# Routing lists of a mixture-of-experts kernel: when the first gathers, the one-hots and the list products are issued

## The chip, the cores and the metric

The kernel runs on one core of one Trainium2 chip. Its time is the device time of one execution in microseconds (us). An execution has five instruction streams: TensorE (PE, with its weight loads as PEld), VectorE (DVE), ScalarE (ACT), GpSimd (POOL) and SyncE (SP, which here only issues transfers). Each stream runs in order; between streams, semaphores make one wait for another.

## The reference

Block-diagonal attention (chunks of 64 positions, 8 heads of 64) makes a matrix x of 4608 tokens by 512. A mixture of 8 experts follows, in which each token goes to one expert only:

```python
logits = x @ w_gate + modality_bias[modality_id]      # 4608 x 8
e_idx = argmax(logits, axis=1)
gate_w = softmax(logits)[arange(N), e_idx]
for e in range(8):
    mask = e_idx == e
    h = maximum(x[mask] @ w1[e], 0)                   # 512 -> 1024
    out[mask] = gate_w[mask, None] * (h @ w2[e])      # 1024 -> 512
```

All is in f32. The matrix products of the experts take three products each, since every factor is split into a high and a low part.

## The kernel before

**Attention.** The tokens come as 36 tiles of 128, worked off in pairs (`a` = 2, 4, ... 34). For a tile, `scores` makes the products of q and k, `exps` and `sums` the softmax, `transposes` and `values` the product with v, and `rows` turns the result back to token rows and makes the logits in the same product; `put` stores the rows to the scratch tensor `xd`. `rows` and `put` of a pair run one pair later than its `values`.

**Slots.** The experts' work is cut into slots: 11 wide ones of 384 tokens (three tiles), then slots of 256. Slots 0 to 12 always run. Slots 13 to 21 stand in nested branches (`rest`) and run only if the routing needs them. Each slot has one expert, and a list says which rows of `xd` belong to it. `gather` fetches these rows by an indirect transfer that POOL issues, one for each tile. For slot 0 the rows are transposed on PE and split (`split`); for later slots they go through a scratch tensor (`stash` and `place`, on SP's queue), DVE transposes blocks of 32 (`turn`), and `part` splits them. A slot has eight slices f = 0 to 7 of the hidden width: `first` makes the hidden slice (PE, then ACT writes its high part hh and DVE its low part hl), `second` adds its product to the output in PSUM. PE runs `first(f)` and then `second(f-1)`, so that hh and hl of a slice have the time of a `second` and a `first` to be made. `wsplit(g+4)` splits the weights of the slice that is four ahead (ACT wh, DVE wl). `finish` scales the outputs and scatters them (POOL).

**Lists.** The tokens are routed in two groups, tiles 0 to 13 (early) and 14 to 35 (late). The early group's lists serve slots 0 to 2 and are made during attention (`early_table`). Tokens of the early group that these slots don't take, and the late group, go into the late lists, for slots 3 and above. A list is made by a matrix product: a one-hot matrix for each tile (`hots`, `late_hots`: POOL compares a row of 0 to 127 with each token's place in its block of 128), times a matrix that has the token's number and gate in the column of its block (a match `eq`, which DVE makes, times `parts`; the lists' products on POOL or DVE). `slot_table` (DVE, some 60 small operations) works out which expert each slot has.

**Order.** The order on each engine is the program's, written by hand. `PLAN` says what is issued after which tile (key -7 is tile 29), `PREP` what is issued in which slice of slots 0 to 2. The routing and the lists are generators in two lists, `jobs` and `pooljobs`. `advance` (line 866) takes each to its next `yield`: first all in `jobs`, then all in `pooljobs`. It is called once for each tile of attention, and in a slot three times a slice: after `first`, after `wsplit`, and after `second` and that slice's `PREP`. Numbered from the start of slot 0, slice f has the advances 3f+1, 3f+2 and 3f+3. The late group's `route` enters the list at advance 1 (its `heads` run then on DVE and POOL); its maximum at advance 3 (`gmx`, line 344), its one-hot `oh` and the prefix sums `scan` at advances 4 and 5 (lines 357 to 366), the gates at 5; then it passes five yields, and the two rank products `rp` (PE, lines 388 and 389) come at advance 10, in slice 3. `slot_table` takes advances 11 to 29, one step each, and `late_lists` follows, with 13 more: in each, a match for four tiles, its product with `parts`, and, four advances behind, four matrix products into `ll` (PE, line 462). `settle` in slice 7 of slot 1 runs down what is left, and `gather 3` follows it.

What an advance issues stands in the engines' in-order streams at that place: PE meets the products `rp` between `first` and `second` of a slice.

Of the kernel before, what the change touches and what calls it, by code (L numbers as in the profile page):

```python
# [26 lines left out]
NT = N // P  # L27
# [3 lines left out]
NTT = SLOT // P  # L31
NWIDE = 11
NSURE = NWIDE + 2
MAXSLOT = 22
BUSY = 4
PLAN = {
    -9: {"fetch": [(0, 1), (1, 1)]},
    -13: {"heads": [(14, 4)]},
    -11: {"heads": [(18, 4)]},
    -7: {"gather": [(0, (0,))], "heads": [(22, 4)]},  # L40
    -6: {"hi": [(0, 0)]},
    -5: {"gather": [(0, (1, 2))], "heads": [(26, 4)], "lo": [(0, 0)], "hi": [(0, 1)]},
    -4: {"fetch": [(2, 1)], "lo": [(0, 1)], "hi": [(1, 0)]},
    -3: {"fetch": [(3, 1)], "heads": [(30, 2)], "lo": [(1, 0)]},
    -2: {"hi": [(1, 1)]},
    -1: {"fetch": [(4,)], "lo": [(1, 1)]},
    0: {"gather": [(1,)], "rank": [()], "hi": [(2,)], "lo": [(2,)]},
}

PREP = {  # L50
# [9 lines left out]
NEARLY = 3  # L60
# [8 lines left out]
NEG = 1  # L69
# [17 lines left out]
C_END = C_TH2 + NJ2  # L87
NBLK = NEARLY * NTT
NTAIL = TAIL // P
NLATE = (NWIDE - NEARLY) * NTT + (MAXSLOT - NWIDE) * NTAIL  # L90
PART = 4


@with_exitstack
def attention_moe(ctx: ExitStack, tc: tile.TileContext, qkv, mod, cst, bias, wcat, wfst, out):
    nc = tc.nc
    V, A, PE, G, SP = nc.vector, nc.scalar, nc.tensor, nc.gpsimd, nc.sync

# [10 lines left out]
    NB, NV = 4, 6  # L109
# [196 lines left out]
    def heads(t0, n, e):  # L306

        a = t0 - GROUPS[1][0]
        l0, lg = lps[1][:, a:a + n], late[:, a:a + n]
        e.tensor_tensor(l0, l0, ris[:, t0:t0 + n].unsqueeze(3).to_broadcast([P, n, H, E]), ALU.mult)  # L310
        lh = wk.tile([P, 4, H // 2, E], F32, name="lh4")[:, 0:n]
        G.tensor_tensor(lh, l0[:, :, 0:4], l0[:, :, 4:8], ALU.add)
        G.tensor_tensor(lh[:, :, 0:2], lh[:, :, 0:2], lh[:, :, 2:4], ALU.add)
        G.tensor_tensor(lg, lh[:, :, 0], lh[:, :, 1], ALU.add)
        G.tensor_tensor(lg, lg, mb[:, t0:t0 + n], ALU.add)
# [4 lines left out]
    def route(g):  # L320
        t0, n = GROUPS[g]
# [60 lines left out]

        if g >= NEG:
            gates()
        for _ in range(2 if g < NEG else 5):
            yield
        rp = ps.tile([P, 2, 32, E], F32, tag="s" if g < NEG else "t", name="rp")
        PE.matmul(rp[:, 0, 0:n], ub, oh, start=True, stop=True)
# [20 lines left out]
            gates()  # L409
            return  # L410
        blocks(pf, pbl[:, ts], blkl[:, ts])
        ready.add("ranks")
        jobs.append(slot_table())

    def blocks(row, low_, high):

        n = row.shape[1]
        pi = wk.tile([P, n], I32, name="pi")
        V.tensor_copy(pi, row)
        V.tensor_single_scalar(pi, pi, P - 1, ALU.bitwise_and)  # L420
        G.tensor_copy(low_, pi)
        G.tensor_tensor(high, row, low_, ALU.subtract)
# [9 lines left out]

    late_hot = []

    def late_hots():

        for t in range(NT):
            if t == n0:
                while "ranks" not in ready:
                    yield  # L440
            if t % 16 == 0:
                b = wk.tile([P, 2, DM], F32, name="qk", bufs=NB).rearrange("p a b -> p (a b)")
                late_hot.append(b.bitcast(BF16).rearrange("p (t b) -> p t b", b=P))
            G.tensor_scalar(late_hot[t // 16][:, t % 16], place_, pbl[:, t:t + 1], None, ALU.is_equal)
            if t % 3 == 2:
                yield
        ready.add("late hot")

    def rank():
        pooljobs.append(late_hots())  # L450

    tkl = cp.tile([P, NLATE], I32, name="tkl")
    gatel = cp.tile([P, NLATE], F32, name="gatel")

    def late_lists(to):

        whats = []
        lt = None

        def product(c):  # L460
            for t in range(c * PART, (c + 1) * PART):
                PE.matmul(lt.rearrange("p b c -> p (b c)"), late_hot[t // 16][:, t % 16],
                          whats[c][:, t % PART], start=(t == 0), stop=(t == NT - 1))

        lag = 4
        for c in range(NT // PART + lag):
            if c < NT // PART:
                tp = slice(c * PART, (c + 1) * PART)
                eq = wk.tile([P, PART, NLATE], BF16, name="eq4")
                V.tensor_tensor(eq, blkl[:, tp].unsqueeze(2).to_broadcast([P, PART, NLATE]),  # L470
                                to.unsqueeze(1).to_broadcast([P, PART, NLATE]), ALU.is_equal)
                w = wk.tile([P, DM], F32, name="v", bufs=NV) if c < NV else wk.tile([P, H, 64], F32, name="ex", bufs=4).rearrange("p a b -> p (a b)")
                w = w.bitcast(BF16)[:, 0:PART * NLATE * 5]
                (V if c % 3 == 2 else G).tensor_tensor(  # L474
                    w.rearrange("p (t b c) -> p t b c", t=PART, c=5),
                    eq.unsqueeze(3).to_broadcast([P, PART, NLATE, 5]),
                    parts[:, tp].unsqueeze(2).to_broadcast([P, PART, NLATE, 5]), ALU.mult)
                whats.append(w.rearrange("p (t m) -> p t m", t=PART))
            if c >= lag:
                if lt is None:  # L480
                    assert "late hot" in ready
                    lt = ps.tile([P, NLATE, 5], F32, tag="t", name="ll")
                product(c - lag)
            yield
        ls = wk.tile([P, NLATE, 5], F32, name="lls", bufs=1)
        V.tensor_copy(ls, lt)
        V.scalar_tensor_tensor(ls[:, :, 0], ls[:, :, 0], float(OOB), ls[:, :, 1], ALU.add, ALU.add)
        V.tensor_copy(tkl, ls[:, :, 0])
        V.tensor_tensor(ls[:, :, 2], ls[:, :, 2], ls[:, :, 3], ALU.add)
        V.tensor_tensor(gatel, ls[:, :, 2], ls[:, :, 4], ALU.add)  # L490
        ready.update(("list", i) for i in range(NEARLY, MAXSLOT))

    taken = cp.tile([P, E], F32, name="taken")

# [3 lines left out]
    def early_table(blk, pf, oh, fm):  # L498
# [49 lines left out]
        V.tensor_tensor(ls[:, :, 2], ls[:, :, 2], ls[:, :, 3], ALU.add)  # L548
        V.tensor_tensor(gate9, ls[:, :, 2], ls[:, :, 4], ALU.add)
        ready.update(("list", i) for i in range(NEARLY))  # L550
        yield
        yield
        gone = wk.tile([P, n0, E], F32, name="gone", bufs=1)
        G.tensor_tensor(gone, oh, taken.unsqueeze(1).to_broadcast([P, n0, E]), ALU.mult)
        first_ = wk.tile([P, n0], F32, name="first", bufs=1)
        V.tensor_scalar(first_, fm, -float(CAP), float(E * CAP), ALU.mult, ALU.add)
        yield
        yield
        left_ = wk.tile([P, n0], F32, name="leftrow", bufs=1)
# [2 lines left out]
        V.tensor_tensor(first_, left_, first_, ALU.is_lt)  # L562
        V.scalar_tensor_tensor(left_, first_, -float(2 ** 20), left_, ALU.mult, ALU.add)
        blocks(left_, pbl[:, 0:n0], blkl[:, 0:n0])

    def slot_table():
        def t1(name, shape):
            return wk.tile([P] + shape, F32, name=name, bufs=1)
# [85 lines left out]
        pn = t1("pn", [W3, NTT])  # L654
        V.tensor_tensor(pn, y[:, 0:W3, E:E + 1].to_broadcast([P, W3, NTT]), bcm(pen, W3, NTT), ALU.mult)
        th3 = thr.rearrange("p (a b) -> p a b", a=NTT)[:, :, 0]
        to = t1("tol", [NLATE])
        for a, r0, r1, m in ((0, 0, W3, NTT), (W3 * NTT, W3, R, NTAIL)):
            V.tensor_tensor(to[:, a:a + (r1 - r0) * m].rearrange("p (a b) -> p a b", b=m),
                            row[:, r0:r1].unsqueeze(2).to_broadcast([P, r1 - r0, m]),  # L660
                            bcm(th3[:, 0:m], r1 - r0, m), ALU.add)
        t3 = to[:, 0:W3 * NTT]
        V.scalar_tensor_tensor(t3, pn.rearrange("p a b -> p (a b)"), -1000.0, t3, ALU.mult, ALU.add)
        jobs.append(late_lists(to))

    def listed(s):
        if s < NEARLY:
# [51 lines left out]
    def split(k, tag="t"):  # L719

        hi, lo = xring[0]
        tp = ps.tile([P, 512], F32, tag=tag, name="tp")[:, 0:SLOT]
        for t in range(NTT):
            assert ("rows", 0, t) in ready
            PE.transpose(tp[:, t * P:(t + 1) * P], xg[:, t, k * P:(k + 1) * P], ident)
        A.copy(hi[:, k], tp)  # L726
        V.tensor_tensor(lo[:, k], tp, hi.bitcast(F32)[:, k], ALU.subtract)  # L727
# [138 lines left out]
    def advance(lists=None):  # L866
        for js in lists or (jobs, pooljobs):
            for j in list(js):
                if next(j, "end") == "end":
                    js.remove(j)  # L870

    ctx.enter_context(tc.manual_schedule())
    ahead = {"rank": rank, "heads": lambda t, n: heads(t, n, G), "gather": gather, "stash": stash, "place": place, "turn": turn, "part": part, "settle": settle, "fetch": fetch, "hi": whi, "lo": wlo, "lo1": wlo}
    def plan(k):
        for what, calls in PLAN.get(k, {}).items():
            for a in calls:
                ahead[what](*a)
# [44 lines left out]
    put(NT - 2)  # L922
    split(2)
    split(3)
    plan(0)

    def last():
# [78 lines left out]
```

## Time and profile before

| | |
|---|---|
| median of three runs | 571.75 us (571.51 to 572.02) |
| profiled execution, device time | 573.04 us |
| its span in the profile | 571.3 us |
| PE busy in the span | 556.2 us (97%) |
| DVE busy | 374.6 us (66%) |
| ACT busy | 244.7 us (43%) |
| POOL busy | 188.2 us (33%) |

The profile is of one execution. Its device time is 1.74 us over its span and 1.29 us over the median of the runs. A row of a timeline gives the start, the duration, engine, line, operation and how many were merged; in brackets stands how long the engine was idle ahead of it and what ended that. A row of the windows gives a stretch, its length, busy time of each engine with its count of instructions, the clock granted to TensorE (1.00 is full), the share of DMA in use and GB/s.

### The profile page before, as it was taken

The numbers are of one execution on the slowest core, as the hardware profiler recorded it, in microseconds if no ns is written. First come the engines' busy times: TensorE is split into PE (matmuls) and PEld (weight loads), VectorE is DVE, ScalarE is ACT, GpSimd is POOL, SyncE is SP. The second block draws the span as 40 slices with busy tenths as digits, with TensorE's granted clock in tenths as the row PEclk, the third lists the DMA queues.
The fourth block names the chain that finished last, engine by engine and source line by source line (L and its number), as shares of the span: only waits on it lengthen the run. The fifth ranks groups of instructions, "written<-read, shape, count | busy, mean of one in ns | idle before, by whom it ended". The sixth has DMA issues, their size and how long they took to land.

```text
span 571.3 us, 12435 instructions
## 1 busy us (share of the span) xinstructions
PE 556.2 (97%) x4950; PEld 502.8 (88%) x4950; DVE 374.6 (66%) x655; ACT 244.7 (43%) x422; POOL 188.2 (33%) x244
## 2 busy tenths in 40 slices
PE   8999999998999899999999999999999999999995
PEld 6999999997889689989899898989989988998894
DVE  4767799886899785565655556565655656556751
ACT  3554555464444233343434434344343444434541
POOL 3322556674899745022040402204040210302011
PEclk9999999998999899999999999999999999999999
DMA  9999998987779428758486766839666573755510
GB/s 332 325 304 303 305 309 286 315 319 262 221 245 290 157 94 246 301 173 279 147 290 203 221 225 180 275 134 306 205 210 232 154 273 126 258 185 180 207 38 26
DMA packets 52755, 130.55 MB, mean 229 GB/s; under 512 B 5198, under 2 KB 22734, under 8 KB 46288
## 3 DMA queue, kind: packets, MB, share of 16 engines
q1 hardware_dynamic: 40864, 100.68, 54.3%
q0 software_dynamic: 5920, 18.88, 8.9%
q10 hardware_dynamic: 5904, 10.11, 4.9%
q8 instruction: 41, 0.67, 0.5%
q14 instruction: 26, 0.21, 0.1%
HBM read 102.12 MB, written 28.05 MB: 228 GB/s over the span
## 4 chain that ended last, share of the span: by engine, by line
issue 49%; PE 28%; POOL 11%; DVE 5%; DMA 5%; ACT 2%; POOLq 0%; ACTq 0%; DVEq 0%
PE yb L793 7%; PE hp L780 7%; POOL xg L685 5%; PE sp L242 4%; PE yb L289 4%; PE xp L277 3%; POOL out L805 3%; PE ap L263 2%; DMA qk<-in_qkv 2%; DMA xg<-xd,tk 1%; DMA v<-in_qkv 1%; DVE eq L470 1%; DVE xr L291 1%; POOL ex L474 1%; ACT ex L251 1%
## 5 line engine op out<-in xcount | busy, mean ns | idle before, releaser
L757 DVE TENSOR_TENSOR wl<-raw,wh 128x1024 fp32r<-128x1024 f32 (+1 forms) x106 | 128.1, 1210 | 33.9 <-ACT wh L753 33.7
L783 ACT ACTIVATE hh<-hp 128x384 fp32r<-128x384 f32 (+1 forms) x104 | 49.4, 475 | 225.7 <-PE hp L780 223.0
L780 PE MATMUL hp<-xh,wh 128*128 128x384 f32 (+1 forms) x416 | 137.0, 329 | 0.0
L780 PE MATMUL hp<-xh,wl 128*128 128x384 f32 (+1 forms) x416 | 136.8, 329 | 0.0
L780 PE MATMUL hp<-xl,wh 128*128 128x384 f32 (+1 forms) x416 | 136.3, 328 | 0.2 <-DVE xl L727 0.2
L784 DVE SCALAR_TENSOR_TENSOR hl<-hp,hh 128x384 fp32r<-128x384 f32 (+1 forms) x104 | 55.6, 534 | 106.4 <-ACT hh L783 106.1
L793 PE MATMUL yb<-wh,hh 128*128 128x512 f32 x296 | 118.3, 400 | 0.3 <-ACT hh L783 0.3
L793 PE MATMUL yb<-wh,hl 128*128 128x512 f32 x296 | 117.4, 397 | 0.0
L793 PE MATMUL yb<-wl,hh 128*128 128x512 f32 x296 | 117.2, 396 | 0.0
L805 POOL DMA_INDIRECT out<-yo,tkl x28 | 28.1, 1002 | 248.7 <-DVE yo L804 243.1
L753 ACT CAST wh<-raw 128x1024 fp32r<-128x1024 f32 (+1 forms) x106 | 108.5, 1025 | 0.2 <-issue 0.2
L780 PEld LDWEIGHTS hp<-xh,wh 128*128 128x128 f32 x416 | 78.4, 188 | 4.3 <-ACT xh L726 0.3
L780 PEld LDWEIGHTS hp<-xl,wh 128*128 128x128 f32 x416 | 78.3, 188 | 4.1 <-DVE xl L727 0.4
L780 PEld LDWEIGHTS hp<-xh,wl 128*128 128x128 f32 x416 | 78.2, 188 | 0.0
L793 PEld LDWEIGHTS yb<-wh,hl 128*128 128x128 f32 x296 | 55.8, 189 | 14.3 <-DVE hl L784 0.5
L793 PEld LDWEIGHTS yb<-wh,hh 128*128 128x128 f32 x296 | 56.0, 189 | 9.7 <-ACT hh L783 0.8
L793 PEld LDWEIGHTS yb<-wl,hh 128*128 128x128 f32 x296 | 55.9, 189 | 9.6
L252 POOL TENSOR_TENSOR sr<-ex 128x256 f32<-128x256 f32 x36 | 26.2, 729 | 63.5 <-ACT ex L251 63.5
L685 POOL DMA_INDIRECT xg<-xd,tkl x28 | 33.9, 1212 | 15.8 <-issue 8.2
L277 PE MATMUL xp<-at,v 64*64 64x64 f32 x1152 | 38.6, 222 | 0.5 <-issue 0.5
L242 PEld LDWEIGHTS sp<-qk 64*64 64x64 f32 x1152 | 35.6, 136 | 3.8 <-DVE sm L256 1.2
L289 PE MATMUL yb<-cs,xt 128*128 128x144 f32 x288 | 38.5, 286 | 0.0
(185 smaller groups left out, 592.8 us busy)
## 6 DMA issues: line engine op xcount, KB each, us to landing
raw<-in_wcat SPq DMA_DIRECT2D x48, 1024.0 KB, 6.5
qk<-in_qkv SPq DMA_DIRECT2D x36, 512.0 KB, 6.0
v<-in_qkv SPq DMA_DIRECT2D x36, 256.0 KB, 4.3
xd<-xr ACTq DMA_DIRECT2D x36, 256.0 KB, 4.6
xs<-xg SPq DMA_DIRECT2D x10, 768.0 KB, 6.8
xq<-xs SPq DMA_DIRECT2D x40, 192.0 KB, 3.7
raw<-in_wfst SPq DMA_DIRECT2D x4, 512.0 KB, 5.3
raw<-in_wfst SPq DMA_DIRECT2D x2, 1024.0 KB, 10.0
```

Source lines behind the costliest of these rows:

```text
L242: PE.matmul(sp[cs_, h, :], b[cs_, 0, hs], b[cs_, 1, hs], start=True, stop=True)
L252: G.tensor_tensor(sring[t % 4][:, :, 0:32], ex[:, :, 0:32], ex[:, :, 32:64], ALU.add)
L277: PE.matmul(xp[hs, p, c * 64:c * 64 + 64], v[hs, vs], at[hs, p, c * 64:c * 64 + 64], start=True, stop=True)
L289: PE.matmul(fp[:, p, 0:GWC], xt[:, p, :], gw[:, p, :], start=True, stop=True)
L685: G.indirect_dma_start(xg[:, t, :], None, xd[0:n, :], bass.IndirectOffsetOnAxis(ap=tk[:, t:t + 1], axis=0), bounds_check=n - 1, oob_is_err ...
L753: A.copy(hi, raw)
L757: (G if pool else V).tensor_tensor(lo, raw, hi.bitcast(F32), ALU.subtract)
L780: PE.matmul(hp, a[:, ks], b[:, k, 0:n], start=(m == 0), stop=(m == 3 * NK - 1))
L783: A.activation(hh[:, 0:n], hp, AF.Relu)
L784: V.scalar_tensor_tensor(hl[:, 0:n], hp, 0.0, hh.bitcast(F32)[:, 0:n], ALU.max, ALU.subtract)
L793: PE.matmul(ys[t], a[:, tsl], b[:, DM:2 * DM], start=(f == 0 and i == 0), stop=(f == NF - 1 and i == 2))
L805: w = G.indirect_dma_start(out, bass.IndirectOffsetOnAxis(ap=tk[:, t:t + 1], axis=0), yo, None, bounds_check=N - 1, oob_is_err=False)
```

## The change

Four things are changed.

1. Slot 0's three gathers are all issued after tile 29 (before: one after tile 29, two after tile 31). To make room, POOL's `heads` of tiles 22 to 25 are issued after tile 27.
2. The early group's remainder (`gone`, `first`, `left`, `blocks`) is issued one advance sooner. Its 14 late one-hots start two advances after that, in attention, in a buffer of their own (the early group's logits, no longer needed); three advances' worth of them (tiles 0 to 8) stands ahead of `gather(1)` in POOL's stream, the other five in slice 0 of slot 0.
3. The late group passes two yields where it passed five, so `rp` comes at advance 7, in slice 2. `slot_table` is run two steps an advance (`pairs`), and its end runs straight into `late_whats`: two matches of 18 tiles each for the 28 blocks of slots 3 to 12, and six products with `parts` (four on POOL, two on DVE). All of it is issued by advance 20, in slice 6 of slot 0. The 22 late one-hots of the late group start at advance 7. The 36 matrix products of the lists are issued in one place, in slice 5 of slot 1, with 140 columns each (before: 230).
4. The lists of slots 13 to 21 are made only in the branch of slot 13, if it is taken.

```diff
 PLAN = {
-    -9: {"fetch": [(0, 1), (1, 1)]},
...
-    -7: {"gather": [(0, (0,))], "heads": [(22, 4)]},
+    -9: {"fetch": [(0, 1), (1, 1)], "heads": [(22, 4)]},
+    -7: {"gather": [(0, (0, 1, 2))]},
...
-    -5: {"gather": [(0, (1, 2))], "heads": [(26, 4)], "lo": [(0, 0)], "hi": [(0, 1)]},
+    -5: {"heads": [(26, 4)], "lo": [(0, 0)], "hi": [(0, 1)]},
...
-    1: {0: ["place 2"], 3: ["turn 2 0"], 4: ["part 2 0", "turn 2 1"], 5: ["part 2 1", "turn 2 2"],
+    1: {0: ["place 2"], 3: ["turn 2 0"], 4: ["part 2 0", "turn 2 1"], 5: ["part 2 1", "turn 2 2", "lists"],
...
+NFIXED = (NWIDE - NEARLY) * NTT + (NSURE - NWIDE) * NTAIL
+NLATE = NFIXED + (MAXSLOT - NSURE) * NTAIL
-PART = 4
+PART = 6
...
-        for _ in range(2 if g < NEG else 5):
+        for _ in range(2):
             yield
         rp = ps.tile([P, 2, 32, E], F32, tag="s" if g < NEG else "t", name="rp")
...
-        ready.add("ranks")
-        jobs.append(slot_table())
+        pooljobs.append(late_hots(t0, n, 0))
+        jobs.append(pairs(slot_table()))
...
+    def pairs(job):
+        for i, _ in enumerate(job):
+            if i % 2:
+                yield
+
+    def late_hots(t0, n, wait):
+        for _ in range(wait):
+            yield
+        for t in range(t0, t0 + n):
+            i = t - t0
+            if not t:
+                b = lps[0].rearrange("p t h e -> p (t h e)")
+            elif t >= n0 and i % 16 == 0:
+                b = wk.tile([P, 2, DM], F32, name="qk", bufs=NB).rearrange("p a b -> p (a b)")
+            late_hot.append(b.bitcast(BF16)[:, i % 16 * P:i % 16 * P + P])
+            G.tensor_scalar(late_hot[t], place_, pbl[:, t:t + 1], None, ALU.is_equal)
+            if i % 3 == 2:
+                yield
+                if t < 6:
+                    yield
...
+    def late_whats(b0, b1):
+        n = b1 - b0
+        eq = wk.tile([P, H, 64], F32, name="ex", bufs=4).rearrange("p a b -> p (a b)")
+        eq = eq.bitcast(BF16)[:, 0:NT * n].rearrange("p (t b) -> p t b", b=n)
+        for a in range(0, NT, NT // 2):
+            tp = slice(a, a + NT // 2)
+            V.tensor_tensor(eq[:, tp], blkl[:, tp].unsqueeze(2).to_broadcast([P, NT // 2, n]),
+                            late_to[0][:, b0:b1].unsqueeze(1).to_broadcast([P, NT // 2, n]), ALU.is_equal)
+            yield
+        whats.clear()
+        for c in range(NT // PART):
+            tp = slice(c * PART, (c + 1) * PART)
+            w = wk.tile([P, DM], F32, name="v", bufs=NV).bitcast(BF16)[:, 0:PART * n * 5]
+            (V if c % 3 == 2 else G).tensor_tensor(
+                w.rearrange("p (t b c) -> p t b c", t=PART, c=5),
+                eq[:, tp].unsqueeze(3).to_broadcast([P, PART, n, 5]),
+                parts[:, tp].unsqueeze(2).to_broadcast([P, PART, n, 5]), ALU.mult)
+            whats.append(w.rearrange("p (t m) -> p t m", t=PART))
+            yield
...
+    def late_lists(b0, b1):
+        lt = ps.tile([P, n, 5], F32, tag="t", name="ll")
+        for t in range(NT):
+            PE.matmul(lt.rearrange("p b c -> p (b c)"), late_hot[t], whats[t // PART][:, t % PART],
+                      start=(t == 0), stop=(t == NT - 1))
...
         ready.update(("list", i) for i in range(NEARLY))
-        yield
-        yield
         gone = wk.tile([P, n0, E], F32, name="gone", bufs=1)
...
         yield
         yield
+        yield
         left_ = wk.tile([P, n0], F32, name="leftrow", bufs=1)
...
         blocks(left_, pbl[:, 0:n0], blkl[:, 0:n0])
+        pooljobs.append(late_hots(0, n0, 2))
...
-        jobs.append(late_lists(to))
+        late_to.append(to)
+        yield from late_whats(0, NFIXED)
...
     split(2)
     split(3)
+    for _ in range(2):
+        advance([pooljobs])
     plan(0)
...
         with tc.If(nslot > s):
+            if s == NSURE:
+                for _ in late_whats(NFIXED, NLATE):
+                    pass
+                late_lists(NFIXED, NLATE)
             slot(s)
```

More of the change, by code (lines that the diff above doesn't have):

```diff
@@ L46 @@
     -1: {"fetch": [(4,)], "lo": [(1, 1)]},
-    0: {"gather": [(1,)], "rank": [()], "hi": [(2,)], "lo": [(2,)]},
+    0: {"gather": [(1,)], "hi": [(2,)], "lo": [(2,)]},
 }
@@ L89 @@
 NTAIL = TAIL // P
-NLATE = (NWIDE - NEARLY) * NTT + (MAXSLOT - NWIDE) * NTAIL
-PART = 4
+NFIXED = (NWIDE - NEARLY) * NTT + (NSURE - NWIDE) * NTAIL
+NLATE = NFIXED + (MAXSLOT - NSURE) * NTAIL
+PART = 6
 @with_exitstack
@@ L433, in attention_moe @@
     late_hot = []
[L435 to L439, printed above, removed]
-                    yield
[L441 to L445, printed above, removed]
-                yield
-        ready.add("late hot")
@@ L449, in rank @@
-    def rank():
-        pooljobs.append(late_hots())
+    def pairs(job):
[16 more added lines that the diff above has]
+                if t < 6:
+                    yield
@@ L452, in attention_moe @@
     tkl = cp.tile([P, NLATE], I32, name="tkl")
     gatel = cp.tile([P, NLATE], F32, name="gatel")
[L455 to L483, printed above, removed]
-            yield
-        ls = wk.tile([P, NLATE, 5], F32, name="lls", bufs=1)
@@ L486, in late_lists @@
+    late_to, whats = [], []
+    def late_lists(b0, b1):
+        n = b1 - b0
+        assert len(whats) == NT // PART and len(late_hot) == NT
+        lt = ps.tile([P, n, 5], F32, tag="t", name="ll")
+        for t in range(NT):
+            PE.matmul(lt.rearrange("p b c -> p (b c)"), late_hot[t], whats[t // PART][:, t % PART],
+                      start=(t == 0), stop=(t == NT - 1))
+        ls = wk.tile([P, NFIXED, 5], F32, name="lls", bufs=1)[:, 0:n]
         V.tensor_copy(ls, lt)
         V.scalar_tensor_tensor(ls[:, :, 0], ls[:, :, 0], float(OOB), ls[:, :, 1], ALU.add, ALU.add)
-        V.tensor_copy(tkl, ls[:, :, 0])
+        V.tensor_copy(tkl[:, b0:b1], ls[:, :, 0])
@@ L489, in late_lists @@
         V.tensor_tensor(ls[:, :, 2], ls[:, :, 2], ls[:, :, 3], ALU.add)
-        V.tensor_tensor(gatel, ls[:, :, 2], ls[:, :, 4], ALU.add)
-        ready.update(("list", i) for i in range(NEARLY, MAXSLOT))
+        V.tensor_tensor(gatel[:, b0:b1], ls[:, :, 2], ls[:, :, 4], ALU.add)
+        ready.update(("list", i) for i in (range(NEARLY, NSURE) if not b0 else range(NSURE, MAXSLOT)))
     taken = cp.tile([P, E], F32, name="taken")
@@ L550, in early_table @@
         ready.update(("list", i) for i in range(NEARLY))
-        yield
-        yield
         gone = wk.tile([P, n0, E], F32, name="gone", bufs=1)
@@ L656, in slot_table @@
         th3 = thr.rearrange("p (a b) -> p a b", a=NTT)[:, :, 0]
-        to = t1("tol", [NLATE])
+        to = cp.tile([P, NLATE], F32, name="tol")
         for a, r0, r1, m in ((0, 0, W3, NTT), (W3 * NTT, W3, R, NTAIL)):
@@ L872, in attention_moe @@
     ctx.enter_context(tc.manual_schedule())
-    ahead = {"rank": rank, "heads": lambda t, n: heads(t, n, G), "gather": gather, "stash": stash, "place": place, "turn": turn, "part": part, "settle": settle, "fetch": fetch, "hi": whi, "lo": wlo, "lo1": wlo}
+    ahead = {"lists": lambda: late_lists(0, NFIXED), "heads": lambda t, n: heads(t, n, G), "gather": gather, "stash": stash, "place": place, "turn": turn, "part": part, "settle": settle, "fetch": fetch, "hi": whi, "lo": wlo, "lo1": wlo}
     def plan(k):
```

## The prediction

> **What bounds the kernel now.** I read the page first, then the stretches of the span, then the time lines of PE, DVE and POOL around each stretch in which PE is idle.
>
> ```profile
> span 571.3 us, 12435 instructions
> PE 556.2 (97%) x4950; PEld 502.8 (88%) x4950; DVE 374.6 (66%) x655; ACT 244.7 (43%) x422; POOL 188.2 (33%) x244
> ```
>
> PE sets the end; what can be won is where PE is idle or slow. The windows show where (the first from the end of one product to the start of the next; the others from a slot's or a step's edge to the next):
>
> ```profile
> 129.94:132.16 2.22, 0.00 (x0) 0.00 (x0) 1.86 (x6) 0.82 (x3) 1.75 (x6) 1.00 1.04 432
> 142.14:174.48 32.34, 32.09 (x160) 28.12 (x159) 30.04 (x75) 14.66 (x23) 30.00 (x40) 1.00 0.78 241
> 148.27:175.28 27.01, 26.76 (x132) 23.36 (x132) 26.02 (x68) 12.12 (x19) 25.89 (x35) 1.00 0.78 247
> 174.48:217.03 42.55, 39.39 (x205) 34.23 (x205) 36.47 (x58) 13.96 (x22) 27.04 (x23) 0.96 0.52 174
> 217.03:250.65 33.62, 33.62 (x169) 30.32 (x169) 19.46 (x26) 13.76 (x22) 6.57 (x6) 1.00 0.68 242
> ```
>
> A slot is 33.62 us where nothing disturbs it (slot 2, last row). Slot 1, in which the late lists are made, takes 42.55: 8.9 too many. And 2.22 are lost before slot 0. In slot 0 itself PE is full, but DVE is nearly so too: 26.02 of 27.01 us. That is the row on which this forecast turns.
>
> ```profile
> 117.83 2.03 PE L277 MATMUL xp<-at,v 64*64 64x64 f32 x64
> 129.55 0.38 PE L725 MATMUL tp<-cs,xg 128*128 128x128 f32 x2
> 132.16 0.44 PE L725 MATMUL tp<-cs,xg 128*128 128x128 f32 x1 [2.23 <-DMA xg<-xd,tk]
> 132.54 1.98 PE L277 MATMUL xp<-at,v 64*64 64x64 f32 x32
> 141.00 1.14 PE L289 MATMUL yb<-cs,xt 128*128 128x144 f32 x8
> 188.50 0.56 PE L462 MATMUL ll<-v,qk 128*128 128x230 bf16 x4 [1.42 <-POOL v L474]
> 190.20 0.89 PE L462 MATMUL ll<-v,qk 128*128 128x230 bf16 x4 [1.13 <-POOL v L474]
> 133.00:134.00 1.00, 1.00 (x26) 1.00 (x24) 0.56 (x1) 0.12 (x1) 0.00 (x0) 0.50 0.96 371
> 134.00:135.00 1.00, 1.00 (x13) 0.82 (x10) 0.00 (x0) 0.44 (x1) 0.00 (x0) 0.50 0.17 55
> 192.00:193.00 1.00, 1.00 (x3) 0.75 (x3) 1.00 (x2) 0.00 (x0) 1.00 (x1) 0.50 0.00 0
> 194.00:195.00 1.00, 1.00 (x8) 0.73 (x7) 1.00 (x2) 0.00 (x0) 1.00 (x1) 1.00 0.00 0
> ```
>
> The first wait is for slot 0's gathered rows, the second for POOL's products. After each the granted clock is 0.50 for some 3.4 us, so a wait of two or three microseconds costs up to 1.7 more.
>
> **The change part by part.** I write R for the end of `rows(35)` on PE, 142.14 before (141.00 + 1.14).
>
> **1. Gathers.**
>
> ```profile
> 115.26 1.27 POOL L685 DMA_INDIRECT xg<-xd,tk  x1 [0.30 <-DMA v<-in_qkv]
> 122.22 1.03 POOL L685 DMA_INDIRECT xg<-xd,tk  x1
> 123.55 1.00 POOL L685 DMA_INDIRECT xg<-xd,tk  x1 [0.30 <-issue]
> 123.55 8.57 DMA xg<-xd,tk
> 138.47 1.05 POOL L685 DMA_INDIRECT xg<-xd,tk  x1 [6.46 <-PE tp L725]
> L444 POOL TENSOR_SCALAR qk<-place,pbl x36: 591/608/1867, 147.0 to 181.5; 128x128 bf16<-128x128 f32 x36
> ```
>
> The last gather landed 8.6 us after its start at 123.55. Issued after the first, the two start at about 116.8 and 118.1, and land by 127 even at that latency, before PE's 129.55. The wait of 2.2 goes, and with it the slow clock: the 32 products `xp` that follow took 1.98 for about 1.1 at full clock. From 129.55 to R are 12.6 us, in which PE has about 8.2 us of work at full clock (64 `xp` 2.03, 16 `yb` 2.1, 12 transposes some 1.9, one `first` 2.1) and 1.0 of waits for xh and xl of the last split that stay; gain 3.4, less 0.2 for the remainder of the early group, which now delays a softmax on DVE. **I take 3.2**; ends 2.2 (idle alone) and 4.3 (all waits). `heads` of tiles 22 to 25 goes into POOL's idle time ahead of 115. What is late next on POOL is `gather(1)`: nine one-hots now stand ahead of it (5.5 us at the median of 0.61 each, 7.6 at 0.84, their mean before: 36 in the 30 us that they held POOL), in the 6.46 us in which POOL waited. So it starts at 136.6 to 138.5, not later than before; its stash and place behind it on SP are needed only in slice 5.
>
> **2. Rank products at advance 7.** Here the change adds a wait.
>
> ```profile
> 142.34 0.68 DVE L291 TENSOR_TENSOR xr<-yb,ris 128x512 f32<-128x512 f32 x1
> 147.10 0.34 DVE L344 TENSOR_REDUCE gmx<-late 128x22 f32<-128x176 f32 x1
> 148.69 0.50 PE L793 MATMUL yb<-wh,hh 128*128 128x512 f32 x1 [0.25 <-ACT hh L783]
> 151.53 0.81 DVE L366 TENSOR_TENSOR scan<-scan 128x176 bf16<-128x176 bf16 x3
> 153.12 0.25 PE L388 MATMUL rp<-oh,ub 128*128 128x176 bf16 x1
> ```
>
> The prefix sums end at 152.34, R + 10.2, and before, `rp` stood after `first(3)`, at 153.12: just behind. Now it stands after `first(2)`, ahead of `second(1)`, which began at 148.69, R + 6.55. DVE's chain from R to the sums can hardly shrink: it waits for POOL's `heads` by 0.14 and then runs without a gap. So `second(1)` and all behind it on PE begin at R + 10.7 (10.2, 0.25 for a POOL that comes later from `gather(1)`, 0.25 for `rp`): **4.15 lost**, and 1.2 for the clock after it (0 to 1.7).
>
> **3. DVE in slot 0.** Work moves into slot 0, ahead of hl of slice 7:
>
> ```profile
> 171.78 0.55 DVE L784 SCALAR_TENSOR_TENSOR hl<-hp,hh 128x384 fp32r<-128x384 f32 x1
> 172.25 0.46 DVE L630 TENSOR_TENSOR sy<-cs,cum 128x304 f32<-128x304 f32 x1
> 177.68 0.56 DVE L638 TENSOR_TENSOR sx<-sy,cs 128x304 f32<-128x304 f32 x1
> 183.91 0.34 DVE L470 TENSOR_TENSOR eq<-blkl,tol 128x184 bf16<-128x184 f32 x1
> 188.48 1.88 DVE L470 TENSOR_TENSOR eq<-blkl,tol 128x184 bf16<-128x184 f32 x1 [2.82 <-POOL v L474]
> L474 DVE TENSOR_TENSOR v<-eq,parts x2: 1116/1116/1117, 190.4 to 196.8; 128x920 bf16<-128x920 bf16 x2
> L474 POOL TENSOR_TENSOR v<-eq,parts x4: 1743/1760/2661, 186.7 to 193.9; 128x920 bf16<-128x920 bf16 x4
> 193.72 1.21 DVE L757 TENSOR_TENSOR wl<-raw,wh 128x1024 fp32r<-128x1024 f32 x1
> ```
>
> The table's steps from `sy` (172.25) to the last (182.99) came after that hl; of these 10.7 us three wl (3.5), two hl (0.9), two yo (1.55) and two parts (1.05) are other work, which leaves 3.7. Two matches of 504 elements: the one of 184 took 0.34, hence 0.7 each (an estimate by size), 1.4. Two products of 840 elements by the 1.12 for 920: 2.05. Together 7.1. hl of slice 7 ended at 172.33, R + 30.2; now at R + 37.5 (7.1 and the 0.25 of POOL). PE wants it at R + 30.55 (172.69, third product of `second(7)`), now 5.35 later: R + 35.9. **1.6 lost**; ends 0 (DVE's idle 1.0 taken up, cheaper matches) and 4 (each match and product waiting a little for POOL). For the clock after it, and POOL's products at the slot's edge, 0.9 (0 to 2). Slot 0 from R: 32.34 + 4.15 + 1.2 + 1.6 + 0.9 = 40.2, **7.9 lost**. Even if no order mattered, DVE has 7.1 us more to do and 1.0 free.
>
> The clock's row is 0.50 after an idle of 2.22 us. [...]
>
> **4. Slot 1.** Its waits go: the operands are ready some 20 us before slice 5. What stays are 36 products.
>
> ```profile
> 196.79 0.98 PE L462 MATMUL ll<-v,qk 128*128 128x230 bf16 x8
> 197.53 0.48 PE L793 MATMUL yb<-wh,hh 128*128 128x512 f32 x1
> ```
>
> Eight took 0.74 (197.53 - 196.79), 0.093 each with 230 columns; with 140 columns 0.056, 36 of them 2.0, and 0.4 for starting and ending. Slot 1: 33.62 + 2.4 = 36.0, **6.5 won**; ends 5.6 (0.093 each) and 7.5.
>
> **5. The branch.** Late gathers are 28: eight slots of three and two of two, so slots 3 to 12 and no more.
>
> ```profile
> L685 POOL DMA_INDIRECT xg<-xd,tkl x28 | 33.9, 1212 | 15.8 <-issue 8.2
> ```
>
> What moves into the branch never runs: nothing.
>
> **The sum.** -3.2 + 7.9 - 6.5 = -1.8. The profiled execution, 573.04, would become 571.2; it lies 1.29 over the median, and against the median 571.75 the forecast is **570.0 us**. Own range by the ends that can meet: 568.0 to 572.0.
>
> **Rivals.**
>
> A. *DVE's load is borne.* The wait for `rp` gives DVE its time back, no clock is lost and hl is not late: only 4.15 to 5 of the 7.9 stay. For it: DVE's slack of 1.0, and each hl has a `second` and a `first` of time. Against: 26.02 of 27.01. Time: 571.75 - 9.7 + 4.9 = 567.0.
>
> B. *No wait at `rp` at all*, since the sums are early: -9.7 and some 1 back, 563. For it: only that a faster `heads` would bring the sums forward. Against: 10.2 us of DVE chain behind R against 6.4 of PE work.
>
> C. *Slower: POOL's products block DVE at the edge of slot 0.* POOL's products now come when its one-hots are done (22 at 0.84 and a gather, 23 us after `rp`: R + 34 or so), just where DVE must make hl of slice 7, wl and the parts of slot 1's rows. The match of 184 elements took 1.88 beside POOL's product and 0.34 without: 1.5 each time. Three such waits on DVE's path ahead of slot 1's first products, 4.5, and a slow clock after them decide from about two waits on: 571.75 - 1.8 + 4.5 = 574.4. Against: wl kept its 1.2 us in that stretch and lengthened POOL's product to 2.66 instead.
>
> [...]
>
> D. *The gathers don't come sooner*: DMA is at its limit there (1.04 in the first window), the earlier gathers push back loads of v, and a wait of like length comes elsewhere in attention: 573.2. Against: all loads land some microseconds ahead of their use.
>
> **How the numbers follow.** Chances: forecast 0.50, A 0.19, B 0.06, C 0.17, D 0.08. A measurement of this kernel can tell 0.2%, 1.14 us, from no change, so faster means below 570.6. The forecast's range gives 0.30 faster, 0.17 within, 0.03 slower; A and B 0.25 faster; C 0.02 within and 0.15 slower; D 0.03 within and 0.05 slower. Sum: 0.55, 0.22, 0.23. The range from 566.0 to 574.2 leaves out B and the upper half of C.
>
> **What would show it.** Right: no wait at line 725; `rp` with an idle of about 4 us ahead of it and a clock of 0.5 behind; DVE without a gap to the end of slot 0; slot 1 of 36 us, with one run of 36 `ll`. Wrong: `rp` without a wait (B); hl of slice 7 in time (A); matches or parts of 1.5 us and more at the edge of slot 0 (C); a new wait for v or q and k (D).

## The result and the profile after

The changed kernel takes 579.46 us (median of six executions, 578.01 to 581.46), against 571.74 (571.07 to 572.61) for the kernel before on the same chip: a ratio of 1.0136 (95% interval 1.0114 to 1.0158). It is **slower by 7.7 us**, where 570.0 was forecast. Its profiled execution took 578.71, with a span of 576.9. That is 5.67 more than the profiled execution before (573.04); that one lay 1.29 above its median, this one 0.75 below, hence the other 2.0. On a second chip the same kernel took 578.03 against 571.95, a ratio of 1.0084 (1.0044 to 1.0125); single executions of the kernel before lay between 570.23 and 578.01 there, so this ratio is not that of the two medians (1.0106).

The page of the changed kernel begins like that of before; PE's work has not changed, only the span has grown.

```profile
span 576.9 us, 12427 instructions
PE 556.8 (97%) x4949; PEld 505.5 (88%) x4950; DVE 370.9 (64%) x647; ACT 244.4 (42%) x422; POOL 181.3 (31%) x242
```

PE's waits, as a list (engine, line, what it waited for; then the total, the count and the longest in us). None of the first four was in the kernel before, which had waits for the gathered rows and for POOL's products instead:

```profile
PE hp L788 <- DVE xl L725: 2.8, 1, 2.8
PE rp L390 <- DVE scan L367: 2.6, 1, 2.6
PE yb L801 <- DVE hl L792: 2.1, 1, 2.1
PE rp L389 <- DVE oh L358: 1.5, 1, 1.5
PE sp L243 <- issue: 1.2, 3, 0.4
```

All four new ones are for DVE. Where they stand, from PE's time line of the changed kernel:

```profile
118.26 0.36 PE L243 MATMUL sp<-qk 64*64 64x64 f32 x5 [0.38 <-issue]
119.02 0.33 PE L243 MATMUL sp<-qk 64*64 64x64 f32 x4 [0.40 <-issue]
119.77 0.21 PE L243 MATMUL sp<-qk 64*64 64x64 f32 x1 [0.42 <-issue]
131.57 0.49 PE L733 MATMUL tp<-cs,xg 128*128 128x128 f32 x3
139.32 1.14 PE L290 MATMUL yb<-cs,xt 128*128 128x144 f32 x8
148.23 0.25 PE L389 MATMUL rp<-oh,ub 128*128 128x176 bf16 x1 [1.45 <-DVE oh L358]
151.03 0.31 PE L390 MATMUL rp<-scan,ones 128*128 128x184 bf16 x1 [2.56 <-DVE scan L367]
151.06 0.78 PE L801 MATMUL yb<-wh,hh 128*128 128x512 f32 x1
179.10 0.50 PE L801 MATMUL yb<-wh,hl 128*128 128x512 f32 x1 [2.13 <-DVE hl L792]
181.85 0.52 PE L788 MATMUL hp<-xh,wh 128*128 128x384 f32 x1
186.57 0.69 PE L788 MATMUL hp<-xl,wh 128*128 128x384 f32 x1 [2.79 <-DVE xl L725]
210.02 1.04 PE L490 MATMUL ll<-v,lp 128*128 128x140 bf16 x14
210.90 1.52 PE L490 MATMUL ll<-v,qk 128*128 128x140 bf16 x22
```

`rows(35)` ends at 140.46 (139.32 + 1.14), the new R. The wait for gathered rows is gone (131.57 has none), and so are the waits for POOL's products: the 36 `ll` stand in one run. The windows of the changed kernel, with the same columns as before, show the price: from R to slot 1, slot 1, slot 2, and single microseconds of slow clock.

```profile
140.46:181.85 41.39, 35.26 (x159) 30.51 (x158) 37.41 (x91) 14.96 (x23) 35.36 (x45) 0.89 0.64 213
181.85:222.79 40.94, 38.15 (x206) 34.47 (x205) 25.58 (x34) 13.55 (x21) 10.87 (x8) 0.94 0.52 173
222.79:256.35 33.56, 33.56 (x169) 30.40 (x168) 19.47 (x26) 13.74 (x22) 6.57 (x6) 1.00 0.67 229
154.00:155.00 1.00, 1.00 (x3) 0.76 (x3) 0.96 (x3) 0.00 (x0) 0.70 (x1) 0.50 1.15 258
180.00:181.00 1.00, 1.00 (x4) 0.71 (x3) 1.00 (x1) 0.19 (x1) 1.00 (x2) 0.50 0.00 0
184.00:185.00 1.00, 0.00 (x0) 0.00 (x0) 1.00 (x1) 0.00 (x0) 0.96 (x1) 1.00 0.00 0
188.00:189.00 1.00, 1.00 (x5) 1.00 (x5) 0.30 (x1) 0.36 (x1) 1.00 (x1) 0.50 0.68 204
```

In slot 1 PE stands still at 184 while DVE is busy for the whole microsecond. With what, and what held it, DVE's and POOL's time lines of the changed kernel show:

```profile
174.37 1.21 DVE L765 TENSOR_TENSOR wl<-raw,wh 128x1024 fp32r<-128x1024 f32 x1
177.57 1.02 DVE L719 STREAM_TRANSPOSE xq<-xq 128x384 f32<-128x384 f32 x2
178.53 0.51 DVE L792 SCALAR_TENSOR_TENSOR hl<-hp,hh 128x384 fp32r<-128x384 f32 x1
178.97 7.07 DVE L765 TENSOR_TENSOR wl<-raw,wh 128x1024 fp32r<-128x1024 f32 x1
185.97 1.01 DVE L725 TENSOR_TENSOR xl<-xq,xh 128x384 fp32r<-128x384 f32 x2
171.16 7.54 POOL L452 TENSOR_SCALAR qk<-place,pbl 128x128 bf16<-128x128 f32 x7
178.67 6.29 POOL L475 TENSOR_TENSOR v<-ex,parts 128x840 bf16<-128x840 bf16 x4
```

One `wl`, 1.2 us elsewhere, takes **7.07**. POOL's four products of the late lists run beside it in a row, from 178.67 to 184.96, and `wl` ends 1.08 later, at 186.04: as if it had begun only when the last product had ended. The parts `xl` that slot 1's first products need stand behind it in DVE's stream. POOL's one-hots (L452) don't hold a `wl` so: the one at 174.37 stood beside seven of them in a row (171.16 to 178.70) and kept its 1.21, and the one-hots took 1.08 each.

### The profile page after: what moved, and what is told of

The parts are those of the page before. It is cut to its first block, busy times and chain, and to the rows that moved or that the text cites. A ratio compares the mean times of both kernels' runs of the same rounds, so it can differ in the third digit from the quotient of the medians.

```text
span 576.9 us, 12427 instructions
## 1 busy us (share of the span) xinstructions
PE 556.8 (97%) x4949; PEld 505.5 (88%) x4950; DVE 370.9 (64%) x647; ACT 244.4 (42%) x422; POOL 181.3 (31%) x242
## 4 chain that ended last, share of the span: by engine, by line
issue 48%; PE 31%; POOL 8%; DVE 7%; DMA 3%; ACT 2%; POOLq 0%; ACTq 0%; DVEq 0%
PE hp L788 8%; PE yb L801 7%; PE sp L243 5%; POOL xg L693 5%; PE yb L290 4%; PE xp L278 3%; POOL out L813 3%; DMA qk<-in_qkv 3%; PE ap L264 2%; DVE wl L765 2%; DVE xr L292 1%; PE yb L171 1%; DVE hl L792 1%; ACT ex L252 0%; DVE ex L247 0%
## 5 line engine op out<-in xcount | busy, mean ns | idle before, releaser
L765 DVE TENSOR_TENSOR wl<-raw,wh 128x1024 fp32r<-128x1024 f32 (+1 forms) x106 | 134.1, 1266 | 36.3 <-ACT wh L761 33.5
L693 POOL DMA_INDIRECT xg<-xd,tkl x28 | 35.1, 1254 | 29.6 <-DVE lls L496 21.3
L243 PE MATMUL sp<-qk 64*64 64x64 f32 x1152 | 38.7, 221 | 1.2 <-issue 1.2
```

The lines of the kernel that those rows point to most:

```text
L243: PE.matmul(sp[cs_, h, :], b[cs_, 0, hs], b[cs_, 1, hs], start=True, stop=True)
L693: G.indirect_dma_start(xg[:, t, :], None, xd[0:n, :], bass.IndirectOffsetOnAxis(ap=tk[:, t:t + 1], axis=0), bounds_check=n - 1, oob_is_err ...
L765: (G if pool else V).tensor_tensor(lo, raw, hi.bitcast(F32), ALU.subtract)
```

## The experiments

They ran on three chips, each with its own runs of the kernel before: 571.97 us for the first four, 571.95 for the next four, 570.81 for the last two. "Slot 1 starts" is the first product of slot 1 on PE (before 174.32, after 181.85), "slot 2 starts" likewise (216.86 and 222.79), and R the end of `rows(35)` (142.14 and 140.46).

### The early gathers alone

```diff
 kernel before
-    -9: {"fetch": [(0, 1), (1, 1)]},
+    -9: {"fetch": [(0, 1), (1, 1)], "heads": [(22, 4)]},
-    -7: {"gather": [(0, (0,))], "heads": [(22, 4)]},
+    -7: {"gather": [(0, (0, 1, 2))]},
-    -5: {"gather": [(0, (1, 2))], "heads": [(26, 4)], ...
+    -5: {"heads": [(26, 4)], ...
```

> The kernel before with only slot 0's three gathers after tile 29 (and the heads of tiles 22 to 25 after tile 27). Theory 1, early gathers starve PE's instruction supply: in the changed kernel PE had 1.9 us of idle put down to issue at 117.9 to 119.8, while the gathers ran; the same gaps of 1 to 2 us stand here at about 118, the wait of 2.2 us for the gathered rows is gone, and rows(35) ends 1.5 to 2 us sooner than 142.1; time 570 (569 to 571). Rival, the gaps come of something else in the change (POOL's earlier remainder of the early group, other code): no gaps at 118, rows(35) ends 3.5 us sooner, time 568 to 568.6.

Measured: **569.67 us**, ratio 0.9962 (0.9941 to 0.9982). From PE's time line:

```profile
129.04 0.49 PE L725 MATMUL tp<-cs,xg 128*128 128x128 f32 x3
137.48 1.14 PE L289 MATMUL yb<-cs,xt 128*128 128x144 f32 x8
184.97 0.56 PE L462 MATMUL ll<-v,qk 128*128 128x230 bf16 x4 [1.40 <-POOL v L474]
```

No wait for the rows at the split's transposes, no gap named "issue" at 118, R at 138.62, and the lists' stalls in slot 1 as before. That early gathers bring such gaps whenever they are issued, which those at 118 to 120 of the changed kernel had suggested, is not so. The rival was right in kind, and some 1 us too low in time. Nothing is given back behind R: slot 0 from R and slot 1 take 32.19 and 42.54 us, as before (32.18 and 42.54). The 3.5 us by which R is sooner are read against one execution of the kernel before, which lay 1.29 above its median; between the medians the gathers are worth 2.3 us here.

### The changed kernel with the gathers put back

```diff
 changed kernel: the three entries of PLAN above, reversed
```

> The changed kernel with the gathers of slot 0 back where they were. Theory 1 (early gathers starve PE's instructions): no gaps at 118, the wait for gathered rows of 2 us and its slow clock are back; rows(35) near 142; everything behind it as in the changed kernel; time within 2 us of the changed kernel's 579.5 (579 to 581). Rival (gaps come of something else): gaps at 118 stay and the wait is back as well; rows(35) near 144, time 582 to 583.

Measured: **578.56 us**, ratio 1.0125 (1.009 to 1.0159): about that of the changed kernel, a little below both ranges. There is no gap named "issue" at 118, and two waits for gathered rows (0.71 and 1.10) are back, as theory 1 said, but R is 140.08 and not near 142: the clock stayed at 1.00 after these waits. Slot 1 starts at 181.12, and the stretched `wl` stands there again, with the same length (177.85, 7.07 us). The early gathers are not what makes the change slow. Nor do they save it anything that could be seen at this size.

### Five yields again

```diff
 changed kernel
-        for _ in range(2):
+        for _ in range(2 if g < NEG else 5):
             yield
         rp = ps.tile(...)
```

> The changed kernel with five yields ahead of the rank products, as before. Theory P, each wait is a loss of its own: the 4 us in front of the rank products and the slow clock after it go, the late products of slot 1's edge stay (POOL's products still block DVE), time 575 to 577. Rival Q, DVE's load decides: what is not waited for at the rank products is waited for at hl of slices 6 and 7, and slot 1 begins when it did, 181.9; time 578 to 580.

Measured: **570.1 us**, ratio 0.9971 (0.994 to 1.0002), some 5 us below the lower of the two ranges. PE, DVE and POOL of this kernel:

```profile
150.91 0.25 PE L389 MATMUL rp<-oh,ub 128*128 128x176 bf16 x1
175.49 0.50 PE L801 MATMUL yb<-wh,hl 128*128 128x512 f32 x1 [4.14 <-DVE hl L792]
178.46 1.10 DVE L725 TENSOR_TENSOR xl<-xq,xh 128x384 fp32r<-128x384 f32 x2
182.60 2.65 DVE L765 TENSOR_TENSOR wl<-raw,wh 128x1024 fp32r<-128x1024 f32 x1 [0.38 <-ACT wh L761]
185.64 2.15 DVE L765 TENSOR_TENSOR wl<-raw,wh 128x1024 fp32r<-128x1024 f32 x1
179.37 7.35 POOL L475 TENSOR_TENSOR v<-ex,parts 128x840 bf16<-128x840 bf16 x4
```

The wait for `rp` is gone, but DVE's load is not: 4.14 us of it come back as a wait for hl of slice 7, so that slot 0 from R still takes 38.55 (41.39 in the changed kernel, 32.18 before). That part of slot 0's loss is DVE's, in whatever place PE meets it. The larger gain is in slot 1, now 36.53 us (178.10 to 214.63), and neither theory had it: the parts were made (178.46 to 179.56) just as POOL's products began, and the two `wl` that met the products had no part behind them that PE waited for. So one line brings back some 8 to 9 us, but about half of that (4.4 in slot 1) by an accident of time.

### The products three slices later

```diff
 changed kernel, ahead of the six products in late_whats
         whats.clear()
+        for _ in range(20):
+            yield
```

> The changed kernel with the six products with parts (four POOL, two DVE) ten advances later, in slices 1 and 2 of slot 1. Theory L, POOL's four products in a row block DVE: the weight operation wl of 7.1 us at the end of slot 0 shrinks to 1.2, the first products of slot 1 no longer wait 2.8 us for xl, and one or two DVE operations of 3 to 7 us turn up beside the products at their new place, in slot 1; time 573 to 577. Rival W, DVE simply has too much to do in slot 0: nothing is stretched at the new place, and the wait for xl shrinks by the 2.1 us of the two products that DVE no longer makes there, no more; time 577 to 578.5.

Measured: **572.0 us**, ratio 1.0013 (0.9988 to 1.0037), 1 us below the range of theory L. Slot 1 starts at 176.81, without a wait for xl. The stretch has moved with the products, into slot 1:

```profile
182.70 7.39 DVE L767 TENSOR_TENSOR wl<-raw,wh 128x1024 fp32r<-128x1024 f32 x1 [0.38 <-ACT wh L763]
182.71 6.30 POOL L477 TENSOR_TENSOR v<-ex,parts 128x840 bf16<-128x840 bf16 x4
192.51 0.50 PE L803 MATMUL yb<-wh,hl 128*128 128x512 f32 x1 [2.50 <-DVE hl L794]
193.07 0.40 PE L803 MATMUL yb<-wl,hh 128*128 128x512 f32 x1
```

Again `wl` ends 1.08 after the last of the four (190.09 against 189.01), in another slot. POOL's row of products is what holds it, as that theory said; there it costs PE 2.50, and no slow clock (the products behind it take 0.40, and the granted clock is 1.00 in each microsecond from 189 to 194).

### The changed kernel once more

No edit: the changed kernel beside the runs that follow.

> The changed kernel again, for a second profile of it. Theory K, the 1.9 us in which PE stood for its instructions at 118 belong to the early gathers in this kernel: they are there again, rows(35) ends at 140.5. Rival, they belong to that one execution, like the missing gaps in the two other kernels with early gathers: PE has no gap at 118, and rows(35) ends at 138 to 139. In both the four of POOL's products in a row hold wl for about 6 us at the edge of slot 0. Time 578 to 580 with the first, 576.5 to 579 with the second.

Measured: **578.03 us**, ratio 1.0084 (1.0044 to 1.0125). R is 139.06, with no gap named "issue" at 118 to 120; `rp` waits 1.49 and 2.55, hl 2.27, xl 2.79, `wl` takes 7.07. As the rival said, the gaps belong to single executions; the four waits belong to the kernel.

### All products on DVE

```diff
 changed kernel
-            (V if c % 3 == 2 else G).tensor_tensor(
+            V.tensor_tensor(
```

> The changed kernel with all six products with parts on DVE (none on POOL), at the same place. Theory L, POOL's products block DVE: wl keeps 1.2 us and no product of slot 1 waits for xl; DVE has 4.1 us more to do ahead of hl of slice 7, so the wait for that hl grows from 2.1 to about 6; slot 1 starts at 184 to 186 but then runs its 36 us; time 575.5 to 578.5. Rival W, DVE's load alone: 4.1 us more of it come on top of everything, time 582 to 584.

Measured: **576.32 us**, ratio 1.0069 (1.0047 to 1.0091).

DVE's and PE's time lines:

```profile
182.28 1.20 DVE L765 TENSOR_TENSOR wl<-raw,wh 128x1024 fp32r<-128x1024 f32 x1
182.41 0.80 PE L801 MATMUL yb<-wh,hl 128*128 128x512 f32 x1 [5.18 <-DVE hl L792]
```

The windows of slot 0 from R and of slot 1:

```profile
139.33:185.56 46.23, 36.26 (x159) 31.14 (x158) 40.77 (x97) 14.96 (x23) 35.96 (x42) 0.86 0.59 191
185.56:221.65 36.09, 36.09 (x206) 32.74 (x204) 20.55 (x31) 13.57 (x21) 6.12 (x6) 0.99 0.64 204
```

With no product on POOL the same `wl` takes 1.20, xl is in time, and slot 1 takes 36.09, the 36.0 that was forecast for it. But the four products are now DVE's (some 4 us at about 1.03 each), and slot 0 from R takes 46.23: hl waits 5.18. That is the time that the theory of the held DVE gave. The block and the load are two troubles, and taking the first away by adding to the second wins little.

### The two yields alone

```diff
 kernel before
-        for _ in range(2 if g < NEG else 5):
+        for _ in range(2):
```

> The kernel before with only the five yields ahead of the rank products made two. Theory P, the wait for the rank products is a loss of its own: PE waits about 4 us ahead of second(1), slow clock behind it, slot 1 starts at 178.5 to 180 in place of 174.3, and the late lists end sooner but no faster; time 575.5 to 577.5. Rival Q, DVE decides and gives it back: DVE is ahead afterwards and slot 1, in which it made PE wait, gets shorter by as much; time 571 to 573.5.

Measured: **575.31 us**, ratio 1.0043 (1.0016 to 1.007). `rp` waits 1.10 and 2.59, and slot 0 from R takes 38.29 where it took 32.18, 6.1 more: 3.7 of waits, and the rest with a mean granted clock of 0.91 in that stretch. That the two yields cost by themselves is right (the time lies 0.2 below theory P's range). The rival has a small part of it: slot 1 takes 41.15 where it took 42.54, so of the 6.1 it gives 1.4 back. In the kernel before, where the table is still worked off a step at a time, the earlier `rp` brings nothing more that pays for it.

### The table a step at a time, and its products on DVE in slot 1

```diff
 changed kernel
-        for _ in range(2):
+        for _ in range(2 if g < NEG else 5):
             yield
...
-        jobs.append(pairs(slot_table()))
+        jobs.append(slot_table())
...
-            (V if c % 3 == 2 else G).tensor_tensor(
+            V.tensor_tensor(
```

> The changed kernel with three things put differently: five yields ahead of the rank products (as before), the slot table one step an advance (as before), so that matches and products fall into slices 1 to 3 of slot 1, and all six products on DVE. Theory: no wait at the rank products, slot 0 from rows(35) 32.2 us as before, no DVE operation blocked, slot 1 of 36 to 36.5 us, rows(35) at 138.5 (140.5 with gaps in PE's instructions); time 561.5 to 564.5. Rival, DVE falls behind in slot 1 (7.6 us more than in an undisturbed slot, and the rest of the table): hl late in slices 2 and 3, 2 to 4 us lost; time 565 to 568.

Measured: **562.98 us**, ratio 0.9825 (0.9776 to 0.9873), the fastest of all and within what was expected. Its windows from R to slot 1 and of slot 1:

```profile
140.00:172.51 32.51, 31.89 (x158) 28.04 (x158) 29.73 (x75) 14.47 (x23) 25.87 (x34) 1.00 0.76 248
172.51:208.37 35.86, 35.86 (x206) 32.51 (x204) 30.08 (x54) 13.81 (x22) 13.54 (x15) 1.00 0.68 218
```

The table, one step an advance, ends in slot 1, and the matches and products follow in its slices 1 to 3, where DVE has room (30.08 of 35.86 busy, with them in it). PE stands full in slot 1, at full clock, and slot 0 takes 32.51 where it took 32.18. What the change wins (the early gathers, the lists in one run, narrower) is all there, without what it lost. Three things were changed at once here; the table's single steps alone were not run.

### POOL's products apart

```diff
 changed kernel, behind each product in late_whats
             yield
+            for _ in range(4 if c % 3 < 2 else 0):
+                yield
```

> The changed kernel with two advances more behind each of POOL's four products of the late lists, so that no two of them stand next to each other in POOL's stream; they reach from slice 6 of slot 0 into slice 1 of slot 1. Theory L (the four products in a row hold DVE's wl until the last of them has ended): no wl of 7 us; each wl, xl or part beside one product takes at most about 2.9 (1.2 and one product of 1.6); the wait for xl at the edge of slot 1 falls from 2.8 to 1 or less, slot 1 to 37 or 38, and the time to 574 to 576. Rival (each product costs its wait wherever it stands, as in the prediction's case C): the four waits of 1.5 us are borne apart, the sum of the waits for hl and xl stays at 5 us or more, and the time stays at 577 to 579. The waits for rp (about 4) and the slow clock after it stay by both.

Measured: **575.57 us**, ratio 1.008 (1.006 to 1.0099).

```profile
168.35 6.14 POOL L452 TENSOR_SCALAR qk<-place,pbl 128x128 bf16<-128x128 f32 x7
174.47 4.73 POOL L475 TENSOR_TENSOR v<-ex,parts 128x840 bf16<-128x840 bf16 x3
187.36 1.63 POOL L475 TENSOR_TENSOR v<-ex,parts 128x840 bf16<-128x840 bf16 x1
174.20 6.09 DVE L767 TENSOR_TENSOR wl<-raw,wh 128x1024 fp32r<-128x1024 f32 x1
181.75 0.69 PE L790 MATMUL hp<-xl,wh 128*128 128x384 f32 x1 [4.30 <-DVE xl L727]
```

The time lies in the range of the theory, but for another reason, so it doesn't speak for it. The edit did not do what it was to do: POOL was behind with its one-hots, nothing else stood between the products in its stream, and three of them still ran in a row. Yet the row gives a third length: three products (4.73) stretch `wl` to 6.09, and it ends 1.09 after the last. Slot 1 kept a wait for xl, of 4.30, and took 42.55 us (176.05 to 218.60), not 37 or 38; DVE's two products now come behind hl of slice 7 (at 180.21 and 188.21), so hl waits 0.39 and not 2.13, and the first of them adds its 1.02 ahead of xl.

### The fastest version with the gathers put back

```diff
 the fastest version (above), with the three entries of PLAN as before
```

> The version with five yields, one table step an advance and all products on DVE in slot 1, with the gathers of slot 0 and the heads of tiles 22 to 25 where the kernel before had them. It prices the earlier gathers where nothing else stalls. If they are worth what rows(35) showed (2 to 3.5 us): the wait at the split's first transposes is back, rows(35) ends 1 to 3 us later, and the time is 565 to 566.5. Rival (their gain is given back by gaps of instruction supply in attention, or the wait is only moved): 562.5 to 563.5, the same as with the early gathers.

Measured: **565.56 us**, ratio 0.9897 (0.987 to 0.9925). The waits for gathered rows are back (0.87 and 1.12), R is 141.79 against 140.00. The time and R are in the ranges of the theory. The early gathers are worth 1.4 us between the two profiled executions (565.28 and 563.86) and 2.6 between the medians, though these are of two chips; set against each chip's own kernel before it is 3.7. In a kernel without other stalls the gain stays, and its size is known to a microsecond or two only.

## Why the prediction was wrong

Its steps, each with what the profiled execution of the changed kernel showed. Slot 1 starts 0.16 earlier here than by the edge that the prediction used, so its 40.2 reads 40.0.

| step | predicted | measured | error |
|---|---|---|---|
| 1. R sooner | 3.2 | 1.68 | +1.5 |
| 2. start of `second(1)` after R | 10.7 | 10.60 | -0.1 |
| 2 and 3. from there to slot 1 | 29.3 | 30.79 | +1.5 |
| 4. slot 1 | 36.0 | 40.94 | +4.9 |
| 5. the branch | 0 | nothing seen | 0 |

Together 7.8, so that slot 2 starts 5.9 later (222.79 against 216.86) where -1.8 was forecast; the later slots take 33.57 each instead of 33.62, which brings the span to 5.6.

**Step 4 failed, and with it a clause of step 3.** The sum let slot 1 run its 36.0 without a wait. "Its waits go" is right of the waits for POOL's products: the 36 `ll` took 2.20 (210.02 to the next `first` at 212.22), where 2.4 was said (2.0 for the products, and 0.4 for starting and ending, an estimate of which 0.2 is left by the 2.20). But the price of POOL's products at the slot's edge was put at a share of 0.9, and the wait of slot 1's first products for xl was in no sum. Measured are 2.79 of wait and, of the 4.9, nearly all of the rest as slow clock: 181.85 to 183 as the tail of the wait for hl, 186.57 to 189.9 after the wait for xl. That was **rival C's mechanism**, at C's place. That the price agrees (4.5 said, 4.9 found) is luck, for C's working was another: not three waits of 1.5, one for each instruction of DVE, but one instruction held through a row of four, 2.79 of wait and the clock. The row also came later than C said (R + 38.2, where R + 34 or so was expected), behind hl of slice 7 and not on it. C was given 0.17. The row that stood against it, a `wl` that "kept its 1.2 us" and stretched POOL's product to 2.66, was a poor witness. There the products stood alone behind their matches, but for the first two (186.68 to 190.14), of which DVE met the second only, so DVE lost no more than one product; the change makes both matches first and leaves four products with nothing between them. That the changed order makes a row was in the diff.

**Step 3** had the mechanism: DVE late with hl of slice 7, 2.13 against 1.6 (its hl ends 38.6 after R, 37.5 forecast). The clock was mis-sized. It stays at 0.50 from before 151 to beyond 155, around and after the wait for `rp`, and again after hl; 1.2 and 0.9 were taken, and 5.16 (30.79 less the 25.63 that the same stretch took before, 148.69 to 174.32) less 2.13 leave 3.0 for both. That DVE's load more than the place of `rp` sets slot 0's end is shown by the run with five yields (no wait at `rp`, 4.14 at hl: of the 9.2 us that slot 0 from R takes more than before, 6.4 stay) and the run with all products on DVE (5.18 at hl).

**Step 2** was right: waits of 1.45 and 2.56 and a `second(1)` 4.05 late, 4.15 forecast. The run with the two yields alone shows the same two waits (1.10, 2.59).

**Step 1** was right in kind. The size came from one execution, and R differs between versions and between executions (140.46 and 139.06 in two of the changed kernel). In the four profiles with the old gathers it is 142.14, 140.08, 139.68 and 141.79, mean 140.9; in the eight with the early ones 137.88 to 140.46, mean 139.1. The difference, 1.8, is a rough figure, below the prediction's lower end (2.2). The waits were 1.5 to 2.2 us in all four, but the slow clock behind them, which the prediction counted in its 3.2, came in the first and the last of the four only; in the other two the granted clock stayed at 1.00. In the profiled execution of the changed kernel some 1.9 us were lost at gaps named "issue" (117.9 to 119.8, PE idle for 1.2 of them).

**Rivals.** A (the load is borne) falls with the waits for hl, B with the waits at `rp`. D (the wait comes elsewhere in attention) falls too: the changed kernel has no wait for v, the run with five yields two, of 0.25 and 0.48, and the gaps named "issue" (some 1.9 us) are not in the second execution of the changed kernel.

## What to carry to other kernels

A step that looks off the critical path is paid on the engine that makes it: before work is moved into an earlier stage, read the busy share of that engine in that stage (DVE had 1 us free in 27, and 7 came in), and not over the span (66%). Where GpSimd and VectorE work at the same time, count how many GpSimd products of two tensors can stand in a row and what stands behind the VectorE instruction that meets them, since the whole row may be its price: here a `wl` of 1.2 us took 7.07 beside a row of four (beside seven one-hots in a row it kept its 1.21). And price a gain of two microseconds from several executions, not one.

## What the runs showed of the hardware

**A whole row held one instruction.** In the changed kernel (twice), with the gathers back, with the products later and with them apart, a `wl` of 1.2 us that met a row of POOL's products ended 1.08 or 1.09 after the last of it, with rows of four (6.29 or 6.30 us) and three (4.73). One product took 1.60 us on average in the changed kernel, so `wl` waited for more than one: up to four went ahead of it. With the products apart `wl` even began first (174.20, the row of three 174.47), beside the last one-hot, and all three went ahead of it. Only the products did this here: beside rows of one-hots every `wl` kept 1.21 to 1.23 in the changed kernel, with five yields and with all products on DVE, and the longest seen elsewhere took 1.35 (the early gathers alone, at 177.47). Nor is it always so with the products: with five yields a `wl` at 182.60 took 2.65 and ended at 185.25, while POOL's four took 7.35 instead of 6.29, so it came in between two of them. Why it did so there, and why one-hots and products differ, is open; no run was made for it.

**Gaps named "issue".** PE stood without a named wait for 0.4 us three times at 118 to 120 in one execution of the changed kernel, once for 1.35 ahead of 120.40 in the fastest version, and not there in another execution of the changed kernel nor in the five other versions with early gathers. The window 118 to 119 had a DMA share of 1.09, but the second execution had 1.05 there without the gaps. That PE stood for its instructions in them was the author's guess, and no run shows it: of the loads that the profile names "instruction" one falls at about 116.4 in both executions of the changed kernel.

**The clock.** In the changed kernel the granted clock was 0.50 from about 149 to 155.7, 179.6 to 183.0 and 186.4 to 189.8, with the waits of 1.45 and 2.56, of 2.13 and of 2.79 us. It took some 5 us (3.0 in slot 0, 2.1 in slot 1) beside 8.9 of waits. The length of a wait alone doesn't decide it: the wait of 2.50 with the products later, and that of 1.54 for gathered rows in the kernel with the two yields alone, were followed by a clock of 1.00, those of 0.87 and 1.12 in the fastest version with the gathers put back by one of 0.50.
